# Batch 0 starts from q, one run of denominators, a kv tile of its own, and new orders of work in a fused linear-attention and gated-MLP kernel

## The chip, the cores and the metric

The kernel runs on one core of a Trainium2 chip. The metric is the device time of one execution in microseconds (us), measured on the chip and given as the median of several runs. One execution of each kernel was also taken with the hardware profiler; its span is some 1.8 us shorter than its time.

## The reference, cut to what matters

Eight batches of eight heads, 576 tokens, 64 values to a head. Linear attention with phi(x) = x + 1 for x > 0 and exp(x) otherwise, which the kernel takes as min(exp(x), max(x, 0) + 1); then a layer of 512 -> 2048 -> 512 with a Swish that has its own beta for each hidden unit.

```python
def phi(x): return np.where(x > 0, x, np.exp(x) - 1.0) + 1.0
q_p, k_p = phi(q), phi(k)
kv  = einsum('bhsd,bhse->bhde', k_p, v);  z = sum(k_p, axis=2)
num = einsum('bhsd,bhde->bhse', q_p, kv)
den = einsum('bhsd,bhd->bhs',  q_p, z)[..., None] + 1e-06
x   = (num / den) as [4608 tokens, 512]
h   = x @ w_in;  g = h / (1 + exp(-beta * h));  out = g @ w_out
```

## The kernel before

The kernel computes the attention of a batch beside the large matmuls of the batch ahead of it. "Hn" is the phase of the 16 groups `x @ w_in` of batch n, "Yn" that of its `g @ w_out`. TensorE (PE) has matmuls in all phases. VectorE (DVE) and ScalarE (ACT) make phi, divide and empty PSUM. SyncE (SP) issues the outputs and two kinds of transposes by DMA: `qTd`, the transposed phi of q, and `xT`, the transposed attention output. GpSimd (POOL) issues the loads that cast to bf16 and casts v into `vaug`.

The parts that the change and the argument touch:

```python
consts = ctx.enter_context(tc.tile_pool(name="consts", bufs=1))
work   = ctx.enter_context(tc.tile_pool(name="work", bufs=2))
# ...
stage = consts.tile([P, 4096], F32, name="stage")
warm  = consts.tile([P, 512], BF16, name="warm")          # 1024 bytes a partition
# ...
for h0 in (0, 2):
    load(nc.sync, k0f, k, 0, h0, 2)                       # k of batch 0 as fp32, in stage
for h0 in (0, 2):
    load(nc.gpsimd, xq[0], q, 0, h0, 2)                   # q of batch 0, cast by GpSimd
# ...
def kv_tile(b):                                           # 1040 bytes a partition, two buffers
    st[b, "kv"] = work.tile([P, 2, 2, 2 * EA], BF16, tag="kv_bd", name="kv_bd")

def q_trans_dma(b):                                       # phi_q -> qTd, two DMA transposes
    st[b, "qTd"] = work.tile([P, 38, G], BF16, tag="qT", name="qTd")
    nc.gpsimd.memset(st[b, "qTd"][:, 36:37], 0.0)
    for hh in range(2):
        st[b, "qTd", "dma"] = nc.sync.dma_start_transpose(
            out=st[b, "qTd"][:, hh * 2 * J : (hh + 1) * 2 * J],
            in_=st[b, "q"][hh * G : (hh + 1) * G].rearrange("p a j c -> p (a j c)"))

def y_out(b, t, yp, c0=0, c1=512, queues=(nc.sync, nc.sync), copier=nc.vector):
    y_sb = work.tile([P, DM], F32, tag="y_sb", name="y_sb", bufs=3)
    copy(copier, y_sb[:, c0:c1], yp[:, c0:c1])            # then two outputs of 64 rows
# ...
kv_tile(0); phi_tile(0, "k"); phi_tile(0, "q")            # first tiles of the pool work
# ... the start: phi of k, then of q; z, kv, denominators, numerators, x, first h groups ...
# side work of batch b, by group of H (sh) and step of Y (sy); n = b + 1, m = n + 1
if b == 1:
    at(sh, 0, lambda: q_trans_dma(2))
    at(sh, 5, lambda: x_trans(1, 4, nc.vector))
    # ...
    at(sh, 2, lambda: load_kq(3, st[2, "qTd", "dma"]), lambda: load_v(3))
at(sh, 8 if b == 1 else 4, lambda: kv_both(n))
for t in range(NT):
    ff = (10 if b == 1 else 5) + 2 * t
    for g, f in ((ff, numer), (ff + 1, x_trans_dma)):
        at(*((sh, g) if g < FC else (sy, g - FC)), lambda t=t, f=f: f(n, t))
at(sy, 0, lambda: phi_all(m, "q"))
at(sy, 2, lambda: q_trans_dma(m), lambda: load_kq(m + 1, st[m, "qTd", "dma"]))
at(sy, 6, lambda: phi_all(m, "k"), lambda: [v_copy(nc.gpsimd, m, pr) for pr in range(2)])
```

## Time and profile before

| | before |
|---|---|
| time, median of the runs beside the changed kernel | 295.68 us (295.58 to 295.7) |
| span of the profiled run | 295.1 us |
| TensorE busy | 285.4 us, 97% |
| dummy matmuls in the start | x27, 9.3 us |
| first real h matmul / first full h group | 15.56 / 21.49 us |
| phi of batch 3's q complete | 80.55 us |
| fourth group of H2 starts (a group is four matmuls of 512 columns) | 87.64 us, after a wait of 0.51 us |

The profiled run itself took 296.92 us, 1.2 more than the median, so the spans of two profiles do not differ by just what the medians do.

The prediction below shows the lines on TensorE and the start; the 1283 ns that it names are the length of the load of Silu's table, which starts at 15.72 us. SyncE's queue in the order of time. The columns are start, duration, engine, source line, operation, out<-in and count.

```profile
80.61 2.83 SPq L260 DMA_TRANSPOSE qTd<-phi_q  x2
83.53 1.38 SPq L359 DMA_DIRECT2D out_dram<-y_sb  x2
84.97 1.25 SPq L318 DMA_TRANSPOSE xT_tail<-xs  x1
86.32 1.18 SPq L359 DMA_DIRECT2D out_dram<-y_sb  x2
```

The reader sees that the first outputs of Y1 can be issued only when the two q transposes have been issued, which takes SyncE 2.83 us, and that the tail of batch 2's xT comes behind the first outputs. Then the DMA view of the whole run: a queue with its packets, its MB and its share of 16 engines' time, and one kind of transfer with its median from issue to landing.

```profile
q1 hardware_dynamic: 37968, 23.48, 34.6%
...
qTd<-phi_q SPq DMA_TRANSPOSE x12, 3.8
```

The 12 q transposes took 3.8 us each to land (median).

### The profile page before, as it was taken

To read this page: it belongs to the slowest core of one execution; us is meant where nothing else is said; L and a number is where in the kernel's file an instruction comes from. 1 tells how busy PE (TensorE), PEld (TensorE's weight loads), DVE (VectorE), ACT (ScalarE), POOL (GpSimd) and SP (SyncE) were. 2 spreads that over 40 slices of the span, in tenths; PEclk is the share of its full clock that TensorE was granted. 3 is DMA by queue.
4 is the path that set the end of the run, shared out by engine and by line. 5 is a ranking of instruction groups with operands and counts; after the bars stand their busy time and mean duration, and the time that the engine had idled before them with its cause. 6 is when DMAs were issued, how large, how long until landed. Compare 5 with 4: busy or idle time off the path is not lost.

```text
span 295.1 us, 4737 instructions
## 1 busy us (share of the span) xinstructions
PE 285.4 (97%) x1859; PEld 143.7 (49%) x1889; DVE 116.1 (39%) x270; ACT 160.1 (54%) x213; POOL 37.3 (13%) x55
## 2 busy tenths in 40 slices
PE   8989999999999999999999999999999999999994
PEld 2674456555445444554455445544554444444443
DVE  4642775844363461356135622653250200110021
ACT  4677756954655781678167906690671077017500
POOL 8632100320022005000500043000000000000000
PEclk9999999999999999999999999999999999999999
DMA  7999999389669939942994299817131310130032
GB/s 217 185 213 394 254 246 189 86 233 212 49 147 241 236 70 265 235 68 56 245 243 73 51 187 270 118 40 159 38 71 44 73 36 0 36 86 22 0 71 74
DMA packets 50903, 40.83 MB, mean 138 GB/s; under 512 B 30768, under 2 KB 42304, under 8 KB 50880
## 3 DMA queue, kind: packets, MB, share of 16 engines
q1 hardware_dynamic: 37968, 23.48, 34.6%
q0 software_dynamic: 12752, 16.91, 29.4%
q8 instruction: 15, 0.25, 0.3%
q10 hardware_dynamic: 160, 0.13, 0.2%
q14 instruction: 8, 0.07, 0.1%
HBM read 36.71 MB, written 9.44 MB: 156 GB/s over the span
## 4 chain that ended last, share of the span: by engine, by line
PE 86%; DMA 6%; ACT 2%; DVE 2%; issue 2%; SPq 0%; POOL 0%; DVEq 0%; POOLq 0%; ACTq 0%
PE y_ps L344 37%; PE h_ps L326 37%; DMA xq<-in_q_dram 4%; PE warm_ps L130 3%; PE nps L277 2%; PE kvp L176 2%; DMA qTd<-phi_q 1%; PE h_ps L511 1%; DMA out_dram<-y_sb 1%; DVE y_sb L234 1%; ACT e L141 1%; PE nps L424 1%; PE kv L187 1%; PE xtp L307 0%; ACT L536 0%
## 5 line engine op out<-in xcount | busy, mean ns | idle before, releaser
L334 ACT ACTIVATE g<-h_ps,beta_c 128x512 bf16<-128x512 f32 x144 | 98.4, 688 | 97.6 <-PE h_ps L326 97.2
L344 PE MATMUL y_ps<-w_out,g 128*128 128x512 bf16 (+3 forms) x587 | 126.2, 370 | 0.6
L326 PE MATMUL h_ps<-xT,w_in 128*128 128x512 bf16 x481 | 113.4, 379 | 1.8 <-DVE y_sb L234 0.7
L344 PEld LDWEIGHTS <-g 128*128 128x128 bf16 x600 | 58.0, 98 | 64.7
L326 PEld LDWEIGHTS <-w_in 128*128 128x128 bf16 x560 | 52.7, 97 | 59.2 <-issue 1.8
L234 DVE COPY y_sb<-y_ps 128x512 f32<-128x512 f32 (+2 forms) x36 | 24.0, 672 | 82.5 <-PE y_ps L344 78.2
L291 DVE TENSOR_TENSOR xs<-nps,rden 128x512 bf16<-128x512 f32 (+1 forms) x36 | 24.7, 689 | 4.4 <-DMA xT<-xs 1.8
L82 POOL DMA_DIRECT2D xk<-in_k_dram x7 | 5.2, 744 | 109.9 <-DMA qTd<-phi_q 80.3
L141 ACT ACTIVATE e<-xq 128x1152 bf16<-128x1152 bf16 (+2 forms) x17 | 18.0, 1100 | 0.5 <-DMA xq<-in_q_dram 0.5
L152 DVE TENSOR_TENSOR phi_q<-e,r 128x1152 bf16<-128x1152 bf16 (+2 forms) x17 | 12.1, 722 | 14.0 <-ACT e L141 13.7
L141 ACT ACTIVATE e<-xk 128x1152 bf16<-128x1152 bf16 x14 | 15.4, 1149 | 0.0
L226 DVE TENSOR_TENSOR kv_bd<-kvp,kvmask 128x260 bf16<-128x260 f32 x12 | 4.6, 424 | 25.1 <-PE kvp L176 25.1
L326 PE MATMUL h_ps<-xT_tail,w_in 128*128 128x512 bf16 x63 | 13.9, 379 | 0.1
L285 DVE TENSOR_SCALAR den<-nps 128x8 f32<-128x8 f32 (+1 forms) x30 | 4.9, 165 | 22.6 <-PE nps L277 22.6
L277 PEld LDWEIGHTS <-qTd 128*128 128x128 bf16 x120 | 9.4, 98 | 7.1
L152 DVE TENSOR_TENSOR phi_k<-e,r 128x1152 bf16<-128x1152 bf16 x16 | 11.5, 752 | 2.7 <-ACT e L141 2.7
L277 PE MATMUL nps<-kv_bd,qTd 128*128 128x130 bf16 x120 | 11.9, 221 | 0.3
L166 POOL CAST vaug<-vf 128x1152 bf16<-128x1152 f32 x10 | 11.2, 1159 | 2.4 <-DMA vf<-in_v_dram 2.4
L141 ACT ACT_TABLE_LOAD x6 | 7.7, 1283 | 6.3 <-DMA xq<-in_q_dram 5.3
L130 PE MATMUL warm_ps<-warm 128*128 128x512 bf16 x27 | 9.3, 509 | 1.6 <-DVE warm L95 1.5
L145 DVE TENSOR_SCALAR r<-xq 128x1152 bf16<-128x1152 bf16 x16 | 6.7, 447 | 3.7 <-DMA xq<-in_q_dram 3.7
L334 ACT ACT_TABLE_LOAD x6 | 7.7, 1283 | 0.1
(77 smaller groups left out, 122.2 us busy)
## 6 DMA issues: line engine op xcount, KB each, us to landing
out_dram<-y_sb SPq DMA_DIRECT2D x70, 128.0 KB, 2.4
vf<-in_v_dram SPq DMA_DIRECT2D x5, 1152.0 KB, 6.3
xk<-in_k_dram POOLq DMA_DIRECT2D x7, 576.0 KB, 10.2
xq<-in_q_dram POOLq DMA_DIRECT2D x7, 576.0 KB, 12.8
g<-in_moe_w_out_dram POOLq DMA_DIRECT2D x2, 1024.0 KB, 17.9
stage<-in_moe_w_out_dram POOLq DMA_DIRECT2D x2, 1024.0 KB, 20.4
w_in<-in_moe_w_in_dram POOLq DMA_DIRECT2D x3, 512.0 KB, 13.4
stage<-in_k_dram SPq DMA_DIRECT2D x2, 576.0 KB, 4.5
```

The source lines that it names most:

```text
L130: nc.tensor.matmul(warm_ps[:, 0:cols], warm[:, 0:P], warm[:, 0:cols], start=True, stop=True)
L141: nc.scalar.activation(st[b, a, pr, "e"][:, :, j0:j1], x[:, :, j0:j1], ACTF.Exp)
L145: nc.vector.tensor_scalar(r, x, 0.0, 1.0, ALU.max, ALU.add)
L152: nc.vector.tensor_tensor(st[b, a][:, pr, j0:j1].rearrange("p j (h d) -> p j h d", h=2), st[b, a, pr, "e"][:, :, j0:j1].rearrange("p h j d ...
L166: eng.tensor_copy(vaug[b % 2][:, pr, :, :, 0:D], src[:, 2 * pr : 2 * pr + 2].rearrange("p h j d -> p j h d"),)
L176: nc.tensor.matmul(ps[hh, pr], st[b, "k"][r, pr, j, :], vaug[b % 2][r, pr, j, :, 0:EA], start=(j == 0), stop=(j == J - 1), skip_group_chec ...
L234: eng.tensor_copy(dst, src)
L277: nc.tensor.matmul(nps[: qs.shape[-1], hh, pr * 2 * EA : (pr + 1) * 2 * EA], qs, st[b, "kv"][:, hh, pr, :], start=True, stop=True, skip_gr ...
L291: nc.vector.tensor_mul(xs[:n].rearrange("p i a d -> p a i d"), num, rd[:, :, :, None].to_broadcast([n, 2, 4, D]),)
L326: nc.tensor.matmul(hp[:, c0:c1], w_in_sb[ff // 4][:, kc, (ff % 4) * P : (ff % 4 + 1) * P], x[:, kc, c0:c1], start=(kc == 0), stop=(kc == K ...
L334: nc.scalar.activation(g_sb[b % 2][:, ff, :], hp, ACTF.Silu, scale=beta_c[:, ff : ff + 1])
L344: nc.tensor.matmul(yp[:, c0:c1], g_sb[b % 2][:, ff, t * P : (t + 1) * P], w_out_sb[i][:, c, c0:c1], start=(ff == 0), stop=(ff == FC - 1), ...
```

## The change

The intent: phi of q is not needed before the denominators, but its transposes are a chain of their own, so load q first and let the transposes run while k arrives. One run of denominator matmuls and reciprocals instead of two takes work off DVE. The second half of batch 0's kv is evacuated by ScalarE into a tile `kv0` of which the rest was cleared at the start; the table for Silu is loaded earlier. In Y0, kv of batch 1 is evacuated ahead of its reciprocals, one output copy goes to ScalarE, and the last numerators go behind phi of batch 2. In H1 the attention of batch 2 starts earlier. The core of the diff:

```diff
-    warm = consts.tile([P, 512], BF16, name="warm")
+    warm = xT[1][:, 0, :]
...
-    k0f = stage[:, 0 : 4 * J * D].rearrange("p (h j d) -> p h j d", h=4, j=J)
+    q0f = stage[:, 0 : 4 * J * D].rearrange("p (h j d) -> p h j d", h=4, j=J)
...
-        load(nc.sync, k0f, k, 0, h0, 2)
+        load(nc.sync, q0f, q, 0, h0, 2)
...
-        load(nc.gpsimd, xq[0], q, 0, h0, 2)
+        load(nc.gpsimd, xk[0], k, 0, h0, 2)
...
+    kv0 = consts.tile([P, 2, 2, 2 * EA], BF16)
+    nc.vector.memset(kv0, 0.0)
...
-    kv_tile(0)
+    st[0, "kv"] = kv0
...
-    phi_step("k", 0, phi_part)
-    phi_step("k", 1, phi_part)
-    idle(14)
...
+    idle(20)
...        (q first: its 16 transposes between dummies, two copies on DVE, two on ScalarE)
+    nc.scalar.activation(tiny[:, 1:2], warm[:, 0:1], ACTF.Silu)
...
-    dens(0, (0, 1), dps)
-    recips(0, 2, P, dps)
...
+    dens(0, range(4), dps)
+    recips(0, 4, P, dps)
...
+            nc.scalar.copy(
+                kv0[r, hh, 1, h * EA : h * EA + D], kvp0[hh][r, P + h * D : P + (h + 1) * D]
+            )
...        (Y0: kv_evac(1) ahead of dens(1); y_sb(1) by ScalarE; numer0(1, 4) last)
-            at(sh, 5, lambda: x_trans(1, 4, nc.vector))
+            at(sh, 8, lambda: x_trans(1, 4, nc.vector))
...
-            at(sh, 8 if b == 1 else 4, lambda: kv_both(n))
+            at(sh, 6 if b == 1 else 4, lambda: kv_both(n))
...
-                ff = (10 if b == 1 else 5) + 2 * t
+                ff = (9 if b == 1 else 5) + 2 * t
```

More of the change, by code (lines that the diff above doesn't have):

```diff
@@ L117 @@
     for i in range(4):
-        for c0, c1 in ((0, 2), (2, KC)) if i == 0 else ((0, KC),):
-            nc.gpsimd.dma_start(
-                out=w_in_sb[i][:, c0:c1], in_=w_in_v[:, c0:c1, i * 512 : (i + 1) * 512]
-            )
+        nc.gpsimd.dma_start(out=w_in_sb[i], in_=w_in_v[:, :, i * 512 : (i + 1) * 512])
     def load_w_out(i):
         nc.gpsimd.dma_start(out=w_out_f[i], in_=w_out_v[:, i * 4 : (i + 1) * 4, :])
+    kv0 = consts.tile([P, 2, 2, 2 * EA], BF16)
+    nc.vector.memset(kv0, 0.0)
     warm_ps = mmps.tile([P, 512], F32, tag="mm", name="warm_ps")
@@ L159, in xin @@
     def xin(b, a, pr):
-        if b == 0 and a == "k":
-            return k0f[:, 2 * pr : 2 * pr + 2]
+        if b == 0 and a == "q":
+            return q0f[:, 2 * pr : 2 * pr + 2]
         return (xk if a == "k" else xq)[b % NX][:, 2 * pr : 2 * pr + 2]
@@ L234, in copy, with q_copy @@
             eng.tensor_copy(dst, src)
+    def q_copy(b, k, t, tp, eng):
+        slots = 1 if t == NT - 1 else 2
+        tp = tp.rearrange("p (t a h i g) -> p t a h i g", a=2, h=2, i=slots, g=G)
+        copy(
+            eng,
+            st[b, "qT"][:, t, :, :, 0 : slots * G].rearrange("p a h n -> p (a h) n"),
+            tp[:, k].rearrange("p a h i g -> p (a h) (i g)"),
+        )
     def q_trans(b, ts, tp, engs):
@@ L240, in q_trans @@
         slots = 1 if ts[0] == NT - 1 else 2
-        tp = tp.rearrange("p (t a h i g) -> p t a h i g", a=2, h=2, i=slots, g=G)
+        tv = tp.rearrange("p (t a h i g) -> p t a h i g", a=2, h=2, i=slots, g=G)
         for k, t in enumerate(ts):
@@ L245, in q_trans @@
                     nc.tensor.matmul(
-                        tp[:, k, pr, :, i, :], st[b, "q"][:, pr, 2 * t + i, :], identity,
+                        tv[:, k, pr, :, i, :], st[b, "q"][:, pr, 2 * t + i, :], identity,
                         is_transpose=True, start=True, stop=True, skip_group_check=True,
@@ L249, in q_trans @@
         for k, (t, eng) in enumerate(zip(ts, engs)):
-            copy(
-                eng,
-                st[b, "qT"][:, t, :, :, 0 : slots * G].rearrange("p a h n -> p (a h) n"),
-                tp[:, k].rearrange("p a h i g -> p (a h) (i g)"),
-            )
+            q_copy(b, k, t, tp, eng)
     def q_trans_dma(b):
@@ L438 @@
     num0ps = num0_pool.__enter__()
-    phi_step("k", 0, phi_part)
-    phi_step("k", 1, phi_part)
-    idle(14)
-    phi_step("k", 0, phi_relu)
-    phi_step("k", 0, phi_min)
     phi_step("q", 0, phi_part)
@@ L448 @@
     phi_step("q", 1, phi_part, 4, J)
-    phi_step("k", 1, phi_relu)
+    idle(20)
+    phi_step("q", 0, phi_relu)
+    phi_step("q", 0, phi_min)
+    phi_step("q", 1, phi_relu)
     for i in range(3):
@@ L455 @@
     load(nc.gpsimd, vb[1], v, 1)
+    phi_step("q", 1, phi_min, 0, 4)
+    phi_step("q", 1, phi_min, 4, J)
+    phi_step("k", 0, phi_part)
+    phi_step("k", 1, phi_part)
+    tps = [misc_bf() for _ in range(2)]
+    for i in range(2):
+        q_trans(0, (2 * i, 2 * i + 1), tps[i], ())
+    phi_step("k", 0, phi_relu)
+    q_copy(0, 0, 0, tps[0], nc.vector)
+    phi_step("k", 0, phi_min)
+    phi_step("k", 1, phi_relu)
+    q_copy(0, 1, 1, tps[0], nc.vector)
     phi_step("k", 1, phi_min)
+    for t in (2, 3):
+        q_copy(0, t - 2, t, tps[1], nc.scalar)
+    nc.scalar.activation(tiny[:, 1:2], warm[:, 0:1], ACTF.Silu)
+    idle(3)
     zt = [num0_tile() for _ in range(2)]
     z_products(0, 0, zt)
-    bps = miscps.tile([P, FC], F32, tag="misc", name="bps")
-    nc.tensor.matmul(bps, beta_row, ident16, is_transpose=True, start=True, stop=True)
-    idle(4)
+    idle(6)
     z_products(0, 1, zt)
-    nc.vector.tensor_copy(beta_s, bps)
-    phi_step("q", 0, phi_relu)
     z_evac(zt)
-    phi_step("q", 0, phi_min)
-    phi_step("q", 1, phi_relu)
-    phi_step("q", 1, phi_min, 0, 4)
-    phi_step("q", 1, phi_min, 4, J)
-    idle(10)
     def q_trans0(t):
@@ L517, in h0_part @@
                 )
-    q_trans0(0)
-    q_trans0(1)
     kv_direct(0, 0, kvp0)
@@ L523 @@
         kv_evac(0, hh, (0,), kvp0)
-    dens(0, (0, 1), dps)
-    recips(0, 2, P, dps)
-    q_trans0(2)
-    q_trans0(3)
+    dens(0, range(4), dps)
+    recips(0, 4, P, dps)
+    kv_direct(0, 1, kvp0)
+    bps = miscps.tile([P, FC], F32, tag="misc", name="bps")
+    nc.tensor.matmul(bps, beta_row, ident16, is_transpose=True, start=True, stop=True)
     numer_part((0, 1), 0)
-    kv_direct(0, 1, kvp0)
-    dens(0, (2, 3), dps)
+    numer_part((2, 3), 0)
     for hh in range(2):
-        kv_evac(0, hh, (1,), kvp0)
-    recips(2, 4, P, dps)
+        for h in range(2):
+            r = slice(h * D, (h + 1) * D)
+            nc.scalar.copy(
+                kv0[r, hh, 1, h * EA : h * EA + D], kvp0[hh][r, P + h * D : P + (h + 1) * D]
+            )
+    nc.scalar.copy(beta_s, bps)
+    hps = [mm_tile("h_ps") for _ in range(4)]
     x_part(0, 0)
     x_part(1, 0)
-    nc.scalar.activation(tiny[:, 1:2], warm[:, 0:1], ACTF.Silu)
     numer_part((0, 1), 1)
-    numer_part((2, 3), 0)
-    hps = [mm_tile("h_ps") for _ in range(4)]
     h0_part(0, 0)
-    x_part(0, 1)
+    x_part(2, 0)
     h0_part(1, 0)
-    x_part(1, 1)
+    x_part(3, 0)
     numer_part((2, 3), 1)
@@ L547 @@
     nc.vector.tensor_add(beta_c, beta_s, beta_m)
+    h0_part(2, 0)
+    x_part(0, 1)
+    h0_part(3, 0)
+    x_part(1, 1)
     h0_part(0, 1)
-    x_part(2, 0)
+    x_part(2, 1)
     h0_part(1, 1)
-    x_part(3, 0)
-    h0_part(2, 0)
-    x_part(2, 1)
-    h0_part(3, 0)
     x_part(3, 1)
@@ L613 @@
         kv_direct(1, pr, kv1)
+    for hh in range(2):
+        kv_evac(1, hh, (0, 1), kv1)
     dens(1, range(NT), dps1)
@@ L616 @@
     recips(4, 5, G, dps1)
-    for hh in range(2):
-        kv_evac(1, hh, (0, 1), kv1)
     y_mm(0, 0, 3, yps[0])
@@ L637 @@
     x_trans(1, 3, nc.vector)
-    numer0(1, 4)
-    for t in (1, 2, 3):
+    phi_part(2, "k", 0, xin(2, "k", 0))
+    y_out(0, 1, yps[1], copier=nc.scalar)
+    phi_part(2, "k", 1, xin(2, "k", 1))
+    for t in (2, 3):
         y_out(0, t, yps[t])
     for pr in range(2):
-        phi_part(2, "k", pr, xin(2, "k", pr))
         phi_relu(2, "q", pr, xin(2, "q", pr))
@@ L646 @@
         phi_relu(2, "k", pr, xin(2, "k", pr))
-    for pr in range(2):
         phi_min(2, "k", pr)
+    numer0(1, 4)
     num0_pool.__exit__(None, None, None)
```

## The prediction

> **What bounds the kernel now.** I read four views in this order: the page (busy time by engine), the stretches with idle TensorE time, the instructions in order of time for the first 21 us, and the chain of waits from 53 to 90 us. The page gives the main fact:
>
> ```profile
> PE 285.4 (97%) x1859; PEld 143.7 (49%) x1889; DVE 116.1 (39%) x270; ACT 160.1 (54%) x213; POOL 37.3 (13%) x55
> L344 PE MATMUL y_ps<-w_out,g 128*128 128x512 bf16 (+3 forms) x587 | 126.2, 370 | 0.6
> L326 PE MATMUL h_ps<-xT,w_in 128*128 128x512 bf16 x481 | 113.4, 379 | 1.8 <-DVE y_sb L234 0.7
> ```
>
> TensorE is busy for 285.4 of 295.1 us. The change removes no real matmul, so it can gain only in TensorE's idle time (295.1 - 285.4 = 9.7 us) and in the 9.3 us of dummy matmuls (L130, x27) that fill the start. The table of stretches says where that time is; columns are stretch, length, busy us by engine, clock, DMA share, GB/s:
>
> ```profile
> 0.00:15.50 15.50, 13.74 (x147) 7.27 (x149) 9.43 (x29) 8.83 (x13) 11.07 (x21) 1.00 1.00 201
> 15.50:21.50 6.00, 5.11 (x85) 4.73 (x83) 2.61 (x9) 4.46 (x11) 1.56 (x3) 1.00 1.24 207
> 33.06:53.66 20.60, 19.83 (x217) 12.24 (x219) 12.76 (x32) 13.67 (x18) 1.95 (x2) 1.00 1.01 207
> 53.66:87.60 33.94, 33.08 (x196) 15.85 (x200) 19.73 (x42) 21.25 (x27) 3.18 (x6) 1.00 0.78 154
> ```
>
> Idle are 0.89 us from 15.5 to 21.5, 0.77 in Y0 with batch 1's attention, and 0.86 in H1, Y1 and the start of H2. All later batches lose about 0.16 us each. So the change plays out before 90 us; what it wins or loses there is passed on to the end by a saturated TensorE. The start itself, in order of time:
>
> ```profile
> 4.50 0.76 DVE L145 TENSOR_SCALAR r<-stage 128x1152 bf16<-128x1152 f32 x1 [2.07 <-DMA stage<-in_k_dram]
> 7.93 1.16 ACT L141 ACTIVATE e<-xq 128x1152 bf16<-128x1152 bf16 x1 [0.23 <-DMA xq<-in_q_dram]
> 9.34 1.26 ACT L141 ACTIVATE e<-xq 128x512 bf16<-128x512 bf16 x2 [0.24 <-DMA xq<-in_q_dram]
> 10.72 0.83 DVE L152 TENSOR_TENSOR phi_q<-e,r 128x512 bf16<-128x512 bf16 x2
> 15.56 0.61 PE L511 MATMUL h_ps<-xT,w_in 128*128 128x128 bf16 x8
> 15.72 1.28 ACT L536 ACT_TABLE_LOAD   x1
> 17.53 0.61 PE L511 MATMUL h_ps<-xT,w_in 128*128 128x128 bf16 x8 [0.45 <-ACT xT L505]
> ```
>
> The reader sees arrivals at 4.5 (first input) and 9.3 us (last), phi of the last at 11.55, first real h matmuls at 15.56, and the table load in ScalarE's chain just there. The chain that ended last, from 76 us:
>
> ```profile
> 79.79 0.76 DVE phi_q L152
> 84.33 2.45 DMA out_dram<-y_sb
> 86.90 0.70 DVE y_sb L234
> 87.64 1.89 PE h_ps L326 x8
> ```
>
> Here H2's fourth h group waits 0.51 us for y_sb(3): that needs one of three y_sb buffers, freed when out of Y1's first tile lands, and SyncE issues this only behind two transposes of batch 3's q, which wait for phi_q at 80.55.
>
> [...] the fp32 load lands in 4.5 us, and the r of an fp32 half costs 0.76 to 0.88 us on DVE, of a bf16 half 0.45. [...] The trace has 1283 ns, and 1.4 us from 15.72 to the next copy at 17.12[...]. [...] the first 14 dummies start 0.43 us apart, later ones take about 0.24, the switch lying between 7 and 8 us.
>
> **The change, part by part.**
> 1. q first, k behind: same bytes on the same queues, so q at 4.5 and 6.5, k at about 7.7 and 9.2. DVE then has r and min of q to 8.35, r of k half 0 to 8.8. TensorE's 20 dummies: 14 x 0.43 from 1.46 gives 7.44, 6 x 0.22 more gives 8.8; then 16 transposes of q, two tiles done at about 9.5. DVE now carries two qT copies (0.42 each, from the row of such a copy) among k's work: copy to 9.95, min to 10.6, r 11.0, copy 11.4, min 12.1. phi of the last half is thus ready at 12.1, against 11.55: **0.55 later**.
> 2. One run of denominators, kv's second half on ScalarE: DVE loses 0.49 (kv_bd pair), 0.42 (den and rden) and 0.17 (beta_s). But the chain before the first xs is now z, z_evac, kv, kv_evac, 16 denominator matmuls (0.8), recips 0.6. From 12.1: z to 12.65, kv to 13.3, denominators 14.05, recips 14.65, numerators, first xs 15.55, x copy 16.2, first h at **about 16.35** against 15.56.
> 3. Silu's table load moves to about 11.6, off this chain, and the four pr=0 x_parts come early, so the h block should run without the 0.45 wait: 8 x 0.45 + 6 x 0.12 + 0.25 = 4.6, end 20.95, against about 20.85 before. **Start in sum: loss 0.1**, error perhaps 0.6 either way. The first w_in slice landed by 15.6 and does not bind.
> 4. kv_bd before the denominators in batch 1: removes the 0.31 wait of TensorE at 48.33. y_sb(1) on ScalarE and xs of tile 4 last on DVE: H1's second group no longer waits for y_sb (0.18 to 0.3). Gain 0.5. ScalarE's first silu starts 0.5 later, at 55.9, done before TensorE needs its buffer at 57.1.
> 5. phi_q(2) loses a 0.62 copy and a 0.61 multiply ahead of it: done 1.2 to 1.35 earlier, so qTd(2), the loads of batch 3 behind it and, with DMA saturated from 64 to 77 us, the arrival of q3. Numerators of batch 2 start one group earlier too.
> 6. The hidden cost: moving them by one group puts xT_tail(2) **ahead** of q3's transposes in SyncE's queue (the order listing shows it), while its xs still follows phi_q(3) on DVE. Call phi_q(3)'s end T (80.55 before). Now xs at T+1.0, tail transpose 1.3, two q transposes 2.9, two outs 1.3, landing 2.4: y_sb(3) ends at T+9.1 instead of T+7.0. Also batch 4's loads, and behind them on GpSimd the vaug casts of batch 3 (87.8 to 90.06 before, T+9.5), come 2.3 later: T+11.8. The kv matmuls that need the second cast started at 90.04, so that was already tight. With T at 80.55 - 1.3 - 0.4 = 78.85, casts end at 90.65, 0.6 later than before.
>
> **Sum:** if part 6 binds, H2 runs 0.6 us later than before, whatever was gained upstream: about 296.3. If it does not bind: -0.5 (part 4) - 0.5 (wait at 87.64) + 0.1 = 294.8. I weight them 6 to 4 and get 295.7; since the start could also be better than my hand schedule, I take 295.6.
>
> **Rivals.**
> - *Start gains outright.* For it: ScalarE has no table load on the chain and DVE has 1.1 us less. Against: k's phi is on the chain and is delayed by copies. It would give 293.8 to 294.6 if SyncE's new order does not bind.
> - *SyncE's queue becomes a wait in H2* (part 6). For it: casts and TensorE met within 0.1 us before. Against: T may move earlier by more than 1.7. It gives 296 to 296.8.
> - *DMA hides any gain in Y0.* Batch 1's v lands 21.6 us after its issue at 21.44, so at 43.0, and is needed at 45.18. A gain below 2 us fits under that; no effect expected.
> - *DVE becomes the bound*: 39% busy; only in 8 to 16 us could it matter.
>
> **Range and chances.** 2% is 5.9 us. The idle time the change can touch is about 2.5 us after 15.5 us and perhaps 1 in the start, and the costs I see are about 1: neither side can reach it. Within 2%: 0.97. Range for 8 in 10: 294.0 to 296.9.
>
> **What the changed profile would show.** Right on 1 and 2: last phi_k about 12.1, first h (the L511 of before) at 16.3. Right on 3: no idle over 0.2 in the h block, and the table load at 11.6. Right on 4: no wait on kv_bd near 48, none on y_sb near 54.8. Right on 5: load of batch 3's k issued at 62.6 rather than 64.4. Right on 6: tail transpose ahead of qTd at 80 us, and a TensorE wait of 1 to 2 us on y_sb or on the vaug cast at 87 to 91. The prediction would be wrong if that wait is missing (then 294 to 295) or if first h starts before 15.3.

## The result and the profile after

| | before | after |
|---|---|---|
| median time | 295.68 us (295.58 to 295.7) | 300.1 us (299.42 to 301.3) |
| ratio | 1 | 1.0155 (95%: 1.0121 to 1.0188) |
| span of the profiled run | 295.1 us | 298.1 us |
| granted clock over that run | 0.998 | 0.994 |

A ratio here is the mean time of one kernel's runs over the mean of the other's of the same rounds, so it is not quite the ratio of the medians. The changed kernel is slower by 1.55%, inside 2% but outside the range that was predicted.

The table of stretches of the changed kernel, in the same stretches as the prediction shows before (stretch, length, busy us of PE, PEld, DVE, ACT and POOL, then clock, DMA share, GB/s):

```profile
0.00:15.50 15.50, 13.44 (x156) 7.48 (x157) 10.29 (x30) 10.39 (x18) 11.49 (x21) 1.00 1.03 213
15.50:21.50 6.00, 5.56 (x83) 4.80 (x81) 1.77 (x7) 3.98 (x10) 1.49 (x2) 1.00 1.24 219
33.06:53.66 20.60, 20.43 (x223) 12.60 (x221) 13.47 (x32) 14.51 (x18) 2.23 (x2) 1.00 1.00 207
53.66:87.60 33.94, 31.46 (x193) 15.10 (x192) 17.18 (x37) 20.02 (x26) 1.64 (x3) 1.00 0.84 148
```

TensorE's idle time shrank from 0.89 to 0.44 us in the second stretch and from 0.77 to 0.17 in the third. In the last it grew from 0.86 to 2.48 us. So the loss is there. The start, in order of time:

```profile
10.20 0.74 DVE L152 TENSOR_TENSOR phi_k<-e,r 128x1152 bf16<-128x1152 bf16 x1
10.99 1.28 ACT L474 ACT_TABLE_LOAD   x1
...
15.19 0.60 PE L521 MATMUL h_ps<-xT,w_in 128*128 128x128 bf16 x8
...
20.50 0.81 PE L331 MATMUL h_ps<-xT,w_in 128*128 128x512 bf16 x3 [0.44 <-ACT g L339]
```

phi of the last input is done at 10.20 + 0.74 = 10.94 us, the table load lies beside other work, and the first full h group starts at 20.50, 0.99 us ahead of before. In this run all this is gain; how much of it is chance is told below. The chain that ended last, from batch 3's q on:

```profile
77.77 0.76 DVE phi_q L152
...
80.83 1.32 SPq L265
...
82.20 2.20 SPq L265
...
84.50 1.43 SPq L364
...
85.97 2.37 DMA out_dram<-y_sb
...
89.21 2.38 PE h_ps L331 x8
```

The two q transposes (L265) now take SyncE 1.32 and 2.20 us, and the first output behind them 1.43. SyncE's queue has batch 2's tail ahead of them now:

```profile
79.57 1.17 SPq L323 DMA_TRANSPOSE xT_tail<-xs  x1
80.83 3.57 SPq L265 DMA_TRANSPOSE qTd<-phi_q  x2
84.50 3.34 SPq L364 DMA_DIRECT2D out_dram<-y_sb  x4
```

TensorE's view of the same moment:

```profile
89.21 2.38 PE L331 MATMUL h_ps<-xT,w_in 128*128 128x512 bf16 x8 [4.09 <-DVE y_sb L234]
```

The fourth group of H2 waits 4.09 us, against 0.51 before, and then the eight matmuls of this group and the next take 2.38 us instead of 1.89: the granted clock reads 1.00 up to 90.4 us, and 0.50 from 90.6 to 93.8 us. The DMA view of the changed kernel has the line that led to the cause:

```profile
q1 hardware_dynamic: 37968, 23.48, 37.6%
...
qTd<-phi_q SPq DMA_TRANSPOSE x12, 4.8
```

A q transpose lands after 4.8 us instead of 3.8. (The queue's share is larger too, with the same packets and bytes, but it does not tell the cases apart: of the runs below, a4 has 35.8% with quick transposes and a2 35.6% with slow ones.) The diff does not touch these transposes. What it moves is their source. In the compiled kernel before, the two buffers of `phi_q` start at 184832 and 189440 bytes in a partition, both multiples of 256. In the changed kernel they start at 182752 and 187360, both 224 bytes past a multiple of 256. Two edits do it: `kv_tile(0)` was the first allocation in the pool `work`, and without it the two kv buffers (1056 bytes each with their padding, 2112 together, that is 8 x 256 + 64) no longer lie ahead of phi; and `kv0` takes 1056 bytes among the constants where `warm` took 1024. Together phi_q moves by -2112 + 32 = -2080 bytes.

### The profile page after: what moved, and what is told of

It reads as the page before. It is cut to its first block, busy times and chain, and to the rows that moved or that the text cites.

```text
span 298.1 us, 4770 instructions
## 1 busy us (share of the span) xinstructions
PE 287.1 (96%) x1890; PEld 144.2 (48%) x1890; DVE 115.9 (39%) x267; ACT 160.2 (54%) x217; POOL 36.9 (12%) x54
## 3 DMA queue, kind: packets, MB, share of 16 engines
q1 hardware_dynamic: 37968, 23.48, 37.6%
## 4 chain that ended last, share of the span: by engine, by line
PE 84%; DMA 8%; SPq 2%; DVE 2%; ACT 1%; issue 1%; POOL 0%; DVEq 0%; POOLq 0%; ACTq 0%
PE y_ps L349 37%; PE h_ps L331 37%; DMA xq<-in_q_dram 4%; PE kvp L176 2%; DMA xk<-in_k_dram 2%; PE nps L282 2%; DMA qTd<-phi_q 2%; SPq L265 1%; PE h_ps L521 1%; ACT e L141 1%; DMA out_dram<-y_sb 1%; DVE y_sb L234 1%; PE kv L187 1%; SPq L364 0%; PE warm_ps L130 0%
## 5 line engine op out<-in xcount | busy, mean ns | idle before, releaser
L331 PE MATMUL h_ps<-xT,w_in 128*128 128x512 bf16 x496 | 115.5, 381 | 4.7 <-DVE y_sb L234 4.1
L234 DVE COPY y_sb<-y_ps 128x512 f32<-128x512 f32 (+2 forms) x35 | 23.4, 673 | 86.0 <-PE y_ps L349 81.0
L82 POOL DMA_DIRECT2D xk<-in_k_dram x9 | 6.7, 749 | 114.4 <-DMA qTd<-phi_q 110.9
L152 DVE TENSOR_TENSOR phi_q<-e,r 128x1152 bf16<-128x1152 bf16 (+2 forms) x17 | 12.1, 722 | 16.3 <-ACT e L141 15.9
L141 ACT ACTIVATE e<-xk 128x1152 bf16<-128x1152 bf16 x16 | 17.9, 1152 | 0.5 <-DMA xk<-in_k_dram 0.4
L141 ACT ACTIVATE e<-xq 128x1152 bf16<-128x1152 bf16 x14 | 15.6, 1156 | 0.1
L130 PE MATMUL warm_ps<-xT 128*128 128x512 bf16 x29 | 8.6, 454 | 1.5 <-DVE xT L95 1.5
L176 PEld LDWEIGHTS <-phi_k 64*128 64x128 bf16 x216 | 7.1, 102 | 3.0 <-issue 2.5
L176 PE MATMUL kvp<-vaug,phi_k 64*128 64x130 bf16 x216 | 8.3, 233 | 0.0
```

Of the source, the lines that this page charges most:

```text
L82: return eng.dma_start(out=dst[:, h0 : h0 + n].rearrange("p h j d -> p h (j d)"), in_=rows.rearrange("(i p) e -> p i e", p=P)[:, h0 : h0 + n],
L130: nc.tensor.matmul(warm_ps[:, 0:cols], warm[:, 0:P], warm[:, 0:cols], start=True, stop=True)
L141: nc.scalar.activation(st[b, a, pr, "e"][:, :, j0:j1], x[:, :, j0:j1], ACTF.Exp)
L152: nc.vector.tensor_tensor(st[b, a][:, pr, j0:j1].rearrange("p j (h d) -> p j h d", h=2), st[b, a, pr, "e"][:, :, j0:j1].rearrange("p h j d ...
L176: nc.tensor.matmul(ps[hh, pr], st[b, "k"][r, pr, j, :], vaug[b % 2][r, pr, j, :, 0:EA], start=(j == 0), stop=(j == J - 1), skip_group_chec ...
L234: eng.tensor_copy(dst, src)
```

## The experiments

Sixteen kernels ran, in five groups; kernels of one group ran on the same chip beside the kernel before (its medians: 295.71, 296.0, 295.8, 296.05 and 296.16). All gave a correct result. In the expectations, "64" stands for the boundary that I first suspected; the last two runs (a6 and a7) showed that it is larger than 128 (sources 64 and 128 bytes past a multiple of 256: 4.7 and 4.6 us to landing, against 3.8 on one).

### What binds at 89 us: order in SyncE's queue, buffer, clock

**e1_tail_back**: the changed kernel, with batch 2's tail transpose put back behind batch 3's q transposes.

```diff
-   for g, f in ((ff, numer), (ff + 1, x_trans_dma)):
+   for g, f in ((ff, numer), (ff + (2 if b == 1 and t == NT - 1 else 1), x_trans_dma)):
```

> The changed kernel with one thing put back: in batch 1's Y phase the tail transpose of batch 2 is issued one step later, so in SyncE's queue it stands behind batch 3's q transposes and the first outs, as in the kernel before. Theory A (the tail ahead of them delays the first out, the y_sb buffer and H2): the wait of TensorE for y_sb in H2 falls from 4.1 to 0.6 us or less, no half-rate stretch follows, and the time is 293.0 to 294.2. Rival B (the second q transpose was slow, 2.2 us, because DMA was more loaded earlier, whatever stands ahead of it): a wait of 2.5 us or more stays, 297 or more.

Measured: 296.59 us (295.79 to 298.5), ratio 1.0035 (0.9993 to 1.0076). TensorE's fourth group of H2 in this run:

```profile
87.46 1.89 PE L331 MATMUL h_ps<-xT,w_in 128*128 128x512 bf16 x8 [1.69 <-DVE y_sb L234]
```

The wait fell from 4.09 to 1.69 us and the matmuls ran at full clock (1.00 granted from 84 to 94 us). So the tail's place in the queue is worth about 2.4 us of the wait (counted from the end of phi of batch 3's q, the y_sb copy that TensorE waits for ends 8.4 us later here and 10.6 in the changed kernel), but 1.7 stay, where either theory alone had asked for less than 0.6 or more than 2.5. The q transposes still took 4.8 us to land.

**e2_own_buffer**: the changed kernel, with a buffer of its own for the fourth output tile of Y1, so that nothing waits for the first output's landing.

```diff
-   y_sb = work.tile([P, DM], F32, tag="y_sb", name="y_sb", bufs=3)
+   if (b, t) == (1, 3):
+       y_sb = stage[:, 0:DM]
+   else:
+       y_sb = work.tile([P, DM], F32, tag="y_sb", name="y_sb", bufs=3)
```

> The changed kernel with SyncE's order kept, but y_sb of batch 1's tile 3 in a buffer of its own (the staging area, free by then), so that this copy no longer waits for an out to land. Theory A: the wait for y_sb goes, but behind it stands the next one: batch 3's vaug casts end at about 91.3 us because GpSimd issues loads held by the q transposes first, so the kv matmuls of H2 wait about 3.4 us at 87 to 90.3, and the time is 297.5 to 299, well above 293.5. Rival (only the y_sb buffer matters): 293.0 to 294.2 and no wait above 0.6 us.

Measured: 300.5 us (299.98 to 300.78), ratio 1.0155 (1.0131 to 1.018), a miss. The time is that of the changed kernel. TensorE ran on past the old wait and met the next one:

```profile
91.18 0.70 PE L176 MATMUL kvp<-vaug,phi_k 64*128 64x130 bf16 x18 [3.57 <-POOL vaug L166]
```

GpSimd casts v behind the issue of batch 4's loads, and these wait for the landing of the same q transposes. So y_sb is one of two waits of nearly equal length (4.09 us; 3.57 and a second one of 0.39) with one cause ahead of both; taking one away shows the other.

**e3_fill_wait**: the changed kernel, with 17 dummy matmuls in the wait, so that the clock stays up.

```diff
+   if b == 2 and ff == 3:
+       fill = numps.tile([P, 2, 512], F32, tag="num", name="nps")
+       for _ in range(17):
+           nc.tensor.matmul(fill[:, 0, :], identity, x[:, 0, :], start=True, stop=True, ...)
```

> The changed kernel with 17 dummy matmuls of 512 columns (about 3.7 us) on TensorE inside the wait of H2, ahead of its fourth group. Theory A2 (1.3 of the loss is the clock that falls to half after 4 us of idleness): the fourth group starts at the same 89.2, its 8 matmuls take 1.89 rather than 2.38 and the kv group 1.23 rather than 2.13, the time falls by 1.0 to 1.4 us, and the runs lie closer together. Rival (those matmuls were slow for another reason, as data arriving): no change, 299.4 to 301.3.

Measured: 298.96 us (298.9 to 299.66), ratio 1.0111 (1.0086 to 1.0135).

```profile
85.20 3.83 PE L673 MATMUL nps<-xT,identity 128*128 128x512 bf16 x16
89.86 1.89 PE L331 MATMUL h_ps<-xT,w_in 128*128 128x512 bf16 x8 [0.83 <-DVE y_sb L234]
91.68 1.23 PE L176 MATMUL kvp<-vaug,phi_k 64*128 64x130 bf16 x36
```

The group starts 0.65 us later than in the changed kernel, where the same 89.2 had been expected, and the kernel still ends 1.1 us earlier (300.1 - 298.96). The granted clock of the profiled run is 0.998, against 0.994 in the changed kernel's. The fall of the clock after the wait of 4.09 us thus cost about 1.1 us by itself, or a little more: from the start of the fourth group to the h group behind kv the changed kernel takes 4.38 us (89.21 to 93.59) and this run 2.98 (89.86 to 92.84), 1.4 less.

**e5_groups_only**: the kernel before with the changed groups of batch 2 alone (x_trans at 8, kv_both at 6, numerators from 9: the last three edits of the diff).

> The kernel before with only the shift of batch 2's attention by one or two h groups (kv at 6, numerators from 9, batch 1's tail at 8), all else as before. Theory A: the tail goes ahead of the q transposes in SyncE's queue here too; phi_q of batch 3 ends at about 80 as before, y_sb of tile 3 ends 10.6 after it at 90.5 to 91, TensorE waits 3 to 4 us for it, and with the clock's fall the time is 298.5 to 301. Rival C (the other parts, which bring H2 forward by 2 us, made the wait): 295.2 to 296.5.

Measured: 298.69 us (298.03 to 300.36), ratio 1.0105 (1.0059 to 1.015).

```profile
89.52 1.89 PE L326 MATMUL h_ps<-xT,w_in 128*128 128x512 bf16 x8 [2.80 <-DVE y_sb L234]
```

These three edits cost 3 us here, with q transposes of the old length (3.7 us). The tail is among them, and the trace points at it: the q transposes start 2.3 us after the end of phi of q (82.59 - 80.28), in the kernel before 0.06 us after it (80.61 - 80.55). The tail's new place hurts by itself as long as the work upstream is as late as before.

### Where the tiles lie

**a1_pad**: the changed kernel and 32 bytes of padding, which brings phi_q to 182784, a multiple of 256. No instruction changes.

```diff
     kv0 = consts.tile([P, 2, 2, 2 * EA], BF16)
+    consts.tile([P, 16], BF16, name="pad")
```

> The changed kernel with 32 unused bytes per partition after kv0, nothing else. The change put 1040 bytes (kv0) in the place of 1024 (the dummies' tile), and every work tile, among them phi_q, qTd and xs, now starts 32 bytes past a multiple of 64; in the kernel before they start on a multiple. Theory B2 (that place makes the q transposes slow: 4.8 us to landing in all four runs of the changed layout, 3.7 to 3.8 in both runs of the old): 3.8 us here, the two issues at 80 us take 2.85 rather than 3.57, the wait for y_sb falls from 4.1 to about 2.7, time 297 to 298.5. Rival (they are slower because of other traffic at that time): 4.8 and about 300 as before.

Measured: **295.44 us** (295.2 to 296.0), ratio 0.9988 (0.9973 to 1.0003). This was better than expected. The two lines that answer to the changed kernel's:

```profile
79.59 2.83 SPq L266 DMA_TRANSPOSE qTd<-phi_q  x2
...
82.51 2.76 SPq L365 DMA_DIRECT2D out_dram<-y_sb  x4
```

```profile
86.66 1.89 PE L332 MATMUL h_ps<-xT,w_in 128*128 128x512 bf16 x8 [0.68 <-DVE y_sb L235]
```

The pair of transposes is back at 2.83 us of SyncE (3.57 in the changed kernel), the four outputs behind it at 2.76 (3.34), the median landing at 3.8 us, and the wait at 0.68 us. With 32 bytes the whole loss of the change is gone.

**a2_before_shift**: the same 32 bytes put into the kernel before, where they take phi_q off the boundary (184864).

> The kernel before with 32 unused bytes ahead of its work tiles, nothing else. Theory B2: the median of a q transpose goes from 3.8 to 4.8 us, the wait for y_sb in H2 from 0.5 to 1.5 to 2.0, the time to 296.5 to 297.5. Rival: 3.8 us and 295.7.

Measured: 299.82 us (299.15 to 300.49), ratio 1.0126 (1.01 to 1.0153), more than expected.

```profile
89.63 3.10 PE L326 MATMUL h_ps<-xT,w_in 128*128 128x512 bf16 x8 [2.33 <-DVE y_sb L234]
```

The kernel before becomes as slow as the changed one, by 32 bytes alone: q transposes of 4.8 us, an issue pair of 3.55, a wait of 2.33 us behind one of 0.48, and a fallen clock (0.83 in the stretch from 84 to 94 us).

**a4_before_shift_dst** and **a5_before_shift_src** split this. In the first, a pad of 32 bytes lies between phi_q and the tiles behind it, so the destination qTd, xs and y_sb move and the source does not. In the second, a pad ahead of the pool moves phi (and kv_bd, e and r beside it) by 32, and one more behind it brings the destination to a multiple of 64.

```diff
     def q_trans(b, ts, tp, engs):               # a4 and a5
         if (b, "qT") not in st:
+            if b == 0:
+                work.tile([P, 16], BF16, tag="pad", name="pad", bufs=1)
...
     rden0 = consts.tile([P, NT, 2, 4], F32)      # a5 alone
+    consts.tile([P, 16], BF16, name="pad0")
```

> The kernel before with the 32 unused bytes placed between phi_q and qT, so that the q transposes' source phi_q stays on a multiple of 64 and their destination qTd (with xs and y_sb behind it) starts 32 past one. Theory dst (the destination's place costs the time): median 4.8 us as with both shifted, time 299 to 300.5. Theory src (the source's place): 3.8 us and 295.5 to 296.2. A part from each: between, 4.2 to 4.5.

> The kernel before with 32 bytes of padding ahead of phi_q and 32 more between phi_q and qTd, so that only the source of the q transposes (with the e, r and phi tiles about it) lies 32 bytes past a multiple of 64, and their destination, xs and y_sb lie on multiples of 64 as before. Theory 'source': the q transposes take 4.8 us to landing (3.8 before), the pair of issues 3.5 (2.8), TensorE waits 2 to 3 us on y_sb near 87 us, time 299.3 to 300.3. Theory 'it takes both, or the place of xs or y_sb': transposes at 3.8, time 295.5 to 296.2.

Measured: a4 295.5 us (295.29 to 295.73), ratio 0.9991 (0.9978 to 1.0005), q transposes 3.8 us. a5 300.71 us (300.15 to 300.82), ratio 1.0155 (1.0129 to 1.018), 4.8 us. The pairs, a4 first:

```profile
79.47 2.81 SPq L262 DMA_TRANSPOSE qTd<-phi_q  x2
```

```profile
81.43 3.56 SPq L262 DMA_TRANSPOSE qTd<-phi_q  x2
```

A destination 32 bytes past the boundary cost nothing; with the source there as well, all of the loss came back. So the source has to lie off its place for the loss. The other tiles that moved with it can be left out as a cause: the instructions of DVE and ScalarE on e, r and phi of batch 3 keep their lengths (r 0.83, phi 0.76, e 2.22 us in the kernel before, in a4 and in a5). Two things remain. a5's destination lies on a multiple of 64 but 64 bytes past one of 256, and so no run has a source off a multiple of 256 with a destination on one: whether the source alone is enough is not shown. And in a4 xs, the source of the xT transposes, lies 32 bytes past as well, at no cost that shows: the tail's transposes of xs land at 2.3 us as before, those of the full tiles at 3.6, within the 2.4 to 3.7 of the runs with xs on a multiple of 256. What is found here holds for the q transposes and not for every DMA transpose.

**a6_before_shift_64** and **a7_before_shift_128**: a2 with 64 and with 128 bytes of padding, since all fast runs had phi_q at a multiple of 256 and all slow ones 32 or 224 bytes past one.

> The kernel before with 64 bytes of padding ahead of its work tiles in place of 32. In every fast run so far the source phi_q started at a multiple of 256 bytes (184832 or 182784), in every slow one 32 or 224 bytes past one (184864, 182752), so the rule could be 64 or 256. [...] Theory '64': transposes 3.8 us to landing, pair 2.8, time 295.5 to 296.2 as the kernel before. Theory '256': transposes 4.5 to 5, pair about 3.5, y_sb waits of 2 to 3 us, 299.3 to 300.7 as with 32 bytes.

> The same with 128 bytes of padding. Theory '64': 3.8 us, 295.5 to 296.2. Theory '256': 4.5 to 5 us, 299.3 to 300.7. A rule of 128 would give the fast figures here and the slow ones with 64 bytes.

Measured: a6 298.38 us (297.91 to 298.5), ratio 1.0078 (1.0054 to 1.0101); a7 298.55 us (297.81 to 300.4), ratio 1.0078 (1.0042 to 1.0114). The q transposes in the DMA view, a6 first and then a7:

```profile
qTd<-phi_q SPq DMA_TRANSPOSE x12, 4.7
```

```profile
qTd<-phi_q SPq DMA_TRANSPOSE x12, 4.6
```

Both are slow, so boundaries of 64 and 128 bytes fall. 256 fits all runs, but so does 512: the phi_q buffers of all fast runs also start on multiples of 512, and no run had one 256 bytes past. The pairs took 3.44 and 3.51 us. The waits on y_sb were 2.07 and 2.08 us, each behind a shorter one. The times are some 1.3 to 2.3 us below those of the shifts by 32 bytes, and so below what I had expected, while the transposes' own figures were as expected. A part of it is the clock: from 84 to 94 us it stayed at 1.00 in a6 and fell to 0.83 in a7's profiled run, whose time was 300.4 us, behind waits of the same length. The four runs of a7 split too: 297.81 and 297.86 us at a granted clock of 1.0 and 0.999, 299.25 and 300.4 us at 0.994. So it is partly chance whether such a wait costs the clock as well.

Why such a source costs time is not shown: no view tells what a transfer fetches, the number of packets is 37968 in all of these runs, and the time to landing does not grow with the distance of the source from the multiple of 256 below it (4.8, 4.7, 4.6 and 4.8 us at 32, 64, 128 and 224 bytes past).

### What the change is worth once the tiles lie right

**a3_tail_pad** is a1 with e1's edit, **e9_pad** is a3 with e2's buffer and with the casts of v ahead of batch 4's loads in GpSimd's queue:

```diff
-   at(sy, 6, lambda: phi_all(m, "k"), lambda: [v_copy(nc.gpsimd, m, pr) for pr in range(2)])
+   if b == 1:
+       at(sy, 1, lambda: [v_copy(nc.gpsimd, m, pr) for pr in range(2)])
+   at(sy, 6, lambda: phi_all(m, "k"))
+   if b > 1:
+       at(sy, 6, lambda: [v_copy(nc.gpsimd, m, pr) for pr in range(2)])
```

> The changed kernel with both put back: the tail transpose behind the q transposes, and the 32 bytes. If these two are the whole loss (theory A with B2): q transposes 3.8 us, wait for y_sb in H2 0.3 to 0.9, time 294.0 to 295.2. If a third cause is left: a wait above 1.2 us and 296 or more.

> The kernel of the run with tail and bytes put back, and two waits more taken away: y_sb of batch 1's tile 3 in the free staging area, and batch 3's vaug casts ahead of batch 4's loads in GpSimd's queue. Theory: no TensorE wait above 0.3 us between 82 and 95 us, H2 starts its kv group at about 87.4, time 293.5 to 294.6. Rival (something else then waits there, such as phi_k or DVE): a wait above 0.5 us, 295 or more.

Measured: a3 294.75 us (294.02 to 295.17), ratio 0.9959 (0.994 to 0.9978); e9 **294.13 us** (294.02 to 294.82), ratio 0.9946 (0.993 to 0.9961). e9's TensorE where the wait was:

```profile
83.77 3.83 PE L332 MATMUL h_ps<-xT,w_in 128*128 128x512 bf16 x17
87.53 1.23 PE L177 MATMUL kvp<-vaug,phi_k 64*128 64x130 bf16 x36
```

There is no bracket and so no wait. But a3's profile has no wait of TensorE in H2 either, so e9's two edits found none left to remove, and the intervals of a3 and e9 overlap: nothing shows that e9 adds to a3. Both beat the kernel before, by 0.4 to 0.5%.

**e4_start_only**: the changed start with the pad, and Y0, H1 and the groups as before (those parts of the diff undone).

> The changed kernel's start alone: all that the change does to Y0, H1 and the groups of batch 2 is undone, and the 32 bytes are in, so that work tiles lie as in the kernel before. If the start gains what the traces show (first full h group at 20.5 to 21.25 against 21.07 to 21.49): 0.2 to 0.9 us, H2's wait for y_sb 0.5 as before, time lower by 0.2 to 0.9. My prediction's hand schedule (start loses 0.1): 295.8 to 296.1 on this chip.

Measured: 295.82 us (295.24 to 295.95), ratio 0.9996 (0.9983 to 1.0009). So the start as a whole is worth nothing that shows in the time. The profile has the first full h group at 20.34 us, the earliest of all runs, but this point moves from run to run with the moment at which the dummies quicken, from 0.43 us apart to about 0.21 (at about 4.4 us in e4, 5.2 in the changed kernel and 7.3 in a1, whose first full h groups start at 20.34, 20.50 and 21.35; the expectations call this the clock of the start, but the granted clock reads 1.00 from 0 to 15.5 us in these profiles, and what is behind it is not shown): with the changed start it lies between 20.34 and 21.35 us in nine profiles (mean 20.99: the changed kernel, e1, e2, e3, a1, a3, e9, e4 and e6), with the old one between 20.85 and 21.49 in seven (mean 21.07). From there to the first matmul of H1 it is 32.17 us in e4, as in the kernel before (21.49 to 53.66), and 31.49 us in the changed kernel (20.50 to 51.99), in e6 (21.06 to 52.55) and in e9 (21.25 to 52.74). The new order in Y0 is thus worth 0.68 us, with little spread.

**e6_after_old_groups_pad**: the changed kernel with the pad and the old groups of batch 2 (5, 8 and 10).

> The changed kernel with the 32-byte pad (295.44 as measured) and with batch 2's attention at its old groups of H1 (x_trans at 5, kv_both at 8, numerators from 10), so that the start and DVE's order in Y0 and H1 are the change's alone. Theory 'the earlier groups cost even at the good place' (the version with only the tail put back and the pad took 294.75): no wait on y_sb above 0.3 in H2, 294.5 to 295.0. Rival 'the groups gain as much as they cost': 295.3 to 296.

Measured: 295.96 us (295.51 to 296.18), ratio 0.9997 (0.9976 to 1.0019). There was no wait on y_sb in H2, but a new one of 1.4 us on batch 1's last xs in H1: the changed order on DVE makes this xs last, and the old group 5 wants it too early. So its time does not measure what I wanted; it shows that the order on DVE and the later x_trans belong together.

**p4_idle14** and **p2_late_table** start from e9_pad. p4 cuts the 20 dummies to 14; p2 puts the load of Silu's table back to its old place.

```diff
-   idle(20)                                                     # p4
+   idle(14)
...
-   nc.scalar.activation(tiny[:, 1:2], warm[:, 0:1], ACTF.Silu)  # p2: from behind the q copies
...                                                             # to behind x_part(1, 0)
+   nc.scalar.activation(tiny[:, 1:2], warm[:, 0:1], ACTF.Silu)
```

> The best kernel so far (both put back, own buffer, early casts) with 14 dummies at the start rather than 20. Theory: q's transposes start at 7.6 to 8.5 us with 20, depending on when the clock comes to full rate (5.2 to 7.4 us in the traces), while phi_q is ready at 8.0; with 14 they start at 8.0 to 8.1 always, so the time falls by 0 to 0.5 us and its spread narrows. Rival: TensorE then idles from 6 to 8 us [...] and the time rises by 0.3 or more.

> The best kernel so far with Silu's table load moved back among the x copies of the start, as in the kernel before. Theory (the load on ScalarE's chain caused the 0.45 wait in the h block of before): a wait of 0.4 to 1.3 us in the h block returns and the time rises by 0.4 to 1.2 us. Rival (the new order hides it): no wait above 0.2, within 0.2 us.

Measured: p4 294.33 us (293.94 to 294.51), ratio 0.9948 (0.9936 to 0.9961), the same as e9_pad. p2 295.12 us (294.84 to 295.68), ratio 0.9985 (0.9971 to 0.9999), 0.8 us more than p4 in the same rounds (p2 keeps the 20 dummies, so this takes p4 to stand for e9_pad), with the wait of 0.6 us of the h block on ScalarE's xT copy back at 17.27 us. In its profile the q transposes started at 7.30 us, against 8.54 in e9_pad's, and the first full h group still came no sooner (21.23 against 21.25). The early table load is worth most of a microsecond; as the start as a whole shows no gain (e4), the rest of it must cost about as much, which no run measures by itself.

## Why the prediction was wrong

The centre was 295.6 with a top of 296.9; measured was 300.1. Point by point:

1. **Start, parts 1 and 2: near the mean of the profiles; this one profile came early.** The last phi_k came at 10.94 us and not 12.1, the first h at 15.19 and not 16.35, even ahead of the 15.3 that was named as a sign of being wrong. Two terms were off. I let the 20 dummies run till 8.8 us; the dummies went from 0.43 us apart to about 0.21 at about 5.2 us in this profile, and the q transposes began at 7.58. In e1, e2 and e3 the transposes began at 8.44, 8.54 and 7.89, so a part is chance: over the nine profiles with the new start the first h comes at 15.69 us in the mean (15.03 to 16.04), over the seven with the old one at 15.14, so 0.55 later, where 0.8 was said. And q's second half landed at 5.94 us where I took 6.5. I forecast a loss of 0.1 us for the start; over all profiles it is a gain of 0.1 (20.99 against 21.07), which is nothing.
2. **Part 3: right.** The h block has no wait but the 0.44 us on ScalarE's g that the kernel before has too, and the table load lies at 10.99, beside other work. p2 shows what that is worth: 0.8 us.
3. **Part 4: right.** I said 0.5 us; the way from the first full h group to H1 is 0.68 shorter. No wait on kv_bd near 48 us and none on y_sb near 54.8; from the start of H1 at 51.99 to 82 us TensorE does not stand still.
4. **Part 5: the figures right, in part by luck.** The DMA share from 64 to 77 us, the stretch called saturated, was 1.23 in the kernel before and is 1.05 here. The load of batch 3's k went out at 62.59 us (62.6 said), and phi of q was done at T = 78.53 (78.85 said). But in a1_pad, with quick transposes, T is 77.29: the gain upstream was larger than predicted, and q's later landing beside the slow transposes, which the prediction did not have, took most of the difference back.
5. **Part 6: the mechanism was right, and this is the step that failed.** The tail did go ahead of the q transposes and the wait on y_sb became the bound. But the term "two q transposes 2.9" was 3.57, and the first output behind them, which I took to be as before, 1.43 where the padded kernel a1 has 0.83. So y_sb(3) ended at T + 10.6 and not at T + 9.1, and TensorE waited 4.09 us where 1 to 2 were said. In a1_pad, the same instructions with the source on the boundary, it ended at T + 9.3 (86.60 - 77.29), close to what I said, though two slips cancel there: my terms add up to 8.9 and not 9.1, they leave out the y_sb copy itself (0.70), and they take 1.3 for the two outputs where only some 0.8 lie ahead of the landing of 2.4, which counts from the start of the second. T itself is 1.24 us later in the changed kernel than in a1_pad: the slow transposes of batch 2 hold back the issue of batch 3's loads (62.59 against 62.17 us), and q lands later still. In the four profiles of the changed order without the pad T is 78.29 to 79.39, in a1, a3 and e9 77.29 to 77.79. I had taken each term's duration from the kernel before and never asked whether the tiles still lay where they had lain. The order listing cannot show this; the addresses in the compiled program would have.
6. **The sum left out the clock.** I counted the wait as time lost and no more. Behind the wait of 4.09 us the clock also went down (0.50 granted from 90.6 to 93.8 us), which e3 measures at 1.1 us of the time and 1.4 us of TensorE's work.

Together, in the two profiled runs: the fourth group of H2 starts at 89.21 us in the changed kernel and at 86.66 in a1_pad, 2.55 later, about half of it from the later T and half from the q transposes and the output behind them. From there to the h group behind kv it is 4.38 us against 3.14 (86.66 to 89.80), and the 1.24 more are the clock's (0.83 granted from 84 to 94 us, against 1.00 in a1). That makes 3.8 us, and the times of the two runs differ by 3.9 (299.88 - 296.0). (The medians differ by 4.7: a1's profiled run was its slowest.) So the place of phi_q accounts for the miss. With the place mended the changed kernel takes 295.44 us, near the predicted 295.6. That is partly luck: 295.6 lay between two outcomes, 296.3 with the wait and 294.8 without, and a1_pad's wait of 0.68 us lies between them too.

The rivals: the start as a gain of its own fell (e4). What the change wins, in Y0 and H1, reaches the end once H2 is cleared (a3, e9). SyncE's queue as the new wait was the right rival, and a second wait of the same length, on the casts of v, stood behind it (e2). DMA hid nothing of Y0's gain: all 0.68 us reached H1. DVE was not the bound: behind the start of the dummies, and apart from y_sb, which itself waited for an output's landing, TensorE waited for DVE 0.3 us at most in the changed kernel. And the chance of 0.97 for "within 2%" held, though the range did not.

What stays open: where the extra time of a transposing DMA with such a source comes from; whether the boundary is 256 or 512 bytes; whether the source alone is enough, with a destination on the boundary; why the transposes of xs do not show it; and whether q's later landing in the changed kernel comes from the slow transposes alone.

## What to carry to other kernels

A diff that adds, removes or reorders allocations moves every tile behind them, and a transfer whose code is untouched can change its cost: compare the start addresses of the sources of DMA transposes before and after (here modulo 256 or 512 bytes: 3.7 to 3.9 us to landing on a multiple, 4.6 to 4.8 off one), and where a transpose has become slower, pad to put its source back. When one wait is taken away and the time stays, look for a second one with the same cause ahead of both before doubting the first. And a wait of TensorE that lets the clock fall costs more than its own length (here about 1.2 us more, behind 4.09).

## What the traces show of transposes, the table load and waits

- The q transposes with sources 32, 64, 128 and 224 bytes past a multiple of 256 (and destinations off one too) took 4.8, 4.7, 4.6 and 4.8 us to land, those with one on it 3.7 to 3.9 (medians of the 12 in a run), and SyncE was held 3.4 to 3.6 us by a pair instead of 2.8. The destination alone 32 bytes off cost nothing (3.8 us), nor did it cost the tail's transposes of xs to have their source there (2.3 us).
- In the changed kernel the copy ahead of the load of Silu's table ends at 10.96 us, the load runs from 10.99 for 1.28, and the next instruction starts at 12.28: on neither side is more than 0.03 us lost.
- Single waits of 1.69 and 2.80 us left the eight matmuls behind them at 1.89 us (e1 and e5, a granted clock of 1.00 from 84 to 94 us); 4.09 us made them 2.38 in the changed kernel (0.83). Of waits that follow each other, 0.48 and then 2.33 us let the clock fall too (a2: 3.10 us for the eight, 0.83), and so did 0.67 and 2.08 (a7: 2.83 us for seven of them, where seven take 1.67 at a clock of 1.00 in e1; 0.83), while 0.49 and 2.07 did not (a6: 1.89, 1.00).
